# Attention and two feed-forward layers on one core: in the first batch, the f32 products with the values take the two heads of a pair in turn

## The chip, the cores and the metric

One core of one Trainium2 chip. The metric is the device time of one execution in microseconds, lower is better; the number of a kernel is the median of its runs.

## The reference, cut to what matters

```python
# q, k, v: (4 batches, 12 heads, 448 tokens, 64), float32
def attention(q, k, v, g_q, g_k):
    q_n, k_n = rmsnorm(q, g_q), rmsnorm(k, g_k)
    scores = q_n @ k_n.transpose(0, 1, 3, 2) / sqrt(64)
    attn = exp(scores - scores.max(-1, keepdims=True))
    attn = attn / (attn.sum(-1, keepdims=True) + 1e-09)
    return attn @ v                      # the product that the change touches

def reference(...):
    x = attention(...).transpose(0, 2, 1, 3).reshape(1792, 768)
    h = x @ moe_w_in                     # 768 -> 2048
    x = (h / (1 + exp(-1.702 * h))) @ moe_w_out
    h = x @ moe2_w_in                    # 768 -> 2048
    return (maximum(h, 0) + alpha * minimum(h, 0)) @ moe2_w_out
```

The weights come as 64-bit floats and are turned into 32-bit ones on the chip, word by word.

## The kernel before, in words

**Staging.** The first batch (6 pairs of heads) goes through its attention while the weights of the first layer are loaded, converted and split into two f16 parts. Loop `first_pairs` takes units 0 and 1 of each pair (which give the first 256 query tokens) and, between them, the steps of `w1i`, the first weight matrix; the loop after `first_x` takes units 2 and 3 (the other 192 query tokens) with the steps of `w1o`, the second matrix, and with `first_in`, the first layer's product (line 680), which is PE's main load there. From then on attention of the next batch (`other_batches`) is interleaved with the first layer of the batch before (`moe1`), and last comes the second layer.

**A unit of attention.** `scores` multiplies queries and keys of the two heads (line 491, in f32 for the first batch; its two heads lie in the two halves of PE's rows and take turns), DVE takes the maximum (line 505), `exponent` runs the exponential on ACT (line 515), `high` makes a diagonal matrix of the reciprocal sums on ACT (line 529), and `low` transposes the probabilities by a product with that diagonal (line 549, 128 columns a time, f32) and copies them out of PSUM with ACT (line 555) into the tile `ptf`.

**The products with the values.** Function `values(P, half)` (line 585) has, in the first batch, four blocks of 128 (the last of 64) keys for each of the two heads of pair P. Head j's weights are 128 keys by 64 value columns, and its output goes to PSUM partitions 64j to 64j + 63 of the one tile `xp` (one buffer, two heads side by side), so the two heads use different halves of PE's columns. Half 0 streams 256 columns a product, half 1 streams 192. Each f32 product is two instructions on PE in the trace, each with a weight load of its own, so a call of `values` shows as 16 matmuls. In the other batches the operands are f16 and there are 11 products a head, 22 matmuls a call. What follows a call in the first batch is a copy on ACT (line 599, half 0) or a split on ACT and DVE (lines 140 and 141, half 1), which reads both heads.

**Order.** Each engine runs its instructions in the order in which they stand in its queue. That order is made when the program is built, by a planner that plays the program through with its own cost of each instruction, taking what is ready in the order of the code. Loads are issued by SP's queue, in order; a load of weights (line 223) waits there until the buffer it writes has been read.

Of the kernel before, what the change touches and what calls it, by code (L numbers as in the profile page):

```python
# [57 lines left out]
def attention_moe_kernel(  # L58
# [17 lines left out]
    nc = tc.nc  # L76
# [61 lines left out]
    def split(dst, src, scale):  # L138

        nc.scalar.activation(out=dst[0], in_=src, func=AF.Copy, scale=scale)  # L140
        nc.vector.scalar_tensor_tensor(  # L141
            out=dst[1], in0=src, scalar=scale, in1=dst[0], op0=ALU.mult, op1=ALU.subtract
        )
# [426 lines left out]
    def values(P, half):  # L570
        b, p = divmod(P, NP)
        vs = preps[P][1]
        pt = pts.pop((P, half))
        if half == 0 or b == 0:
            xps[P] = ps_x.tile([128, S], F32, tag="x", name="xp")
        xp = xps[P]
        if b == 0:
            steps = [(c, c, slice(64 if c == 3 else 0, 128)) for c in range(NV)]
        else:
            steps = [(c, c, slice(0, 128)) for c in range(7)] + [(c + 7, c, slice(0, 128)) for c in range(4)]  # L580
        parts = PARTS[half]
        for group in (parts,) if b else [(part,) for part in parts]:
            for i, (c, kc, ks) in enumerate(steps):
                for j, o, t, n in group:
                    nc.tensor.matmul(  # L585
                        out=xp[64 * j:64 * j + 64, t:t + n],
                        lhsT=vs[ks, j, c],
                        rhs=pt[ks, kc, o:o + n],
                        start=(i == 0),
                        stop=(i == len(steps) - 1),  # L590
                    )
        if b and half == 0:
            xs[b, p] = big.tile([128, 2, S], F16, tag="x", name="x", bufs=NX)
        elif b:
            x = xs[b, p]
            split((x[:, 0], x[:, 1]), xp, scales["w1i"][1][:, p:p + 1])
        elif half == 0:
            xraw[p] = big.tile([128, S], F32, tag="x", name="xraw", bufs=NX)
            nc.scalar.activation(out=xraw[p][:, 0:FIRST], in_=xp[:, 0:FIRST], func=AF.Copy)
        else:  # L600
            first_split(p, xp, slice(FIRST, S))

    def first_split(p, src, cols):
        x = xs[0, p]
        split((x[:, 0, cols], x[:, 1, cols]), src[:, cols], first_sc[:, p:p + 1])
# [9 lines left out]
    def attention(us):  # L615

        for i in range(len(us) + LAG):
            if 0 < i <= len(us):
                high(us[i - 1])
            if i < len(us):  # L620
                scores(us[i])
                exponent(us[i])
            if 2 <= i <= len(us) + 1:
                low(us[i - 2])
            if i >= LAG and us[i - LAG] % 2 == 1:
                values(us[i - LAG] // 4, us[i - LAG] % 4 // 2)
            yield
# [476 lines left out]
    if True:  # L1104
# [10 lines left out]
        parts = stage[:, 0:R1I * 1024].bitcast(I32).rearrange("p (i n t) -> p i n t", i=R1I, t=2)  # L1115
# [40 lines left out]
        steps = attention([4 * P + r for P in range(NP) for r in range(2, 4)])  # L1156
# [71 lines left out]
```

## Time and profile before

| | |
|---|---|
| median of 3 runs | 1199.72 us (1193.25, 1199.72, 1202.79) |
| profiled execution | 1196.5 us |
| its span, first to last instruction | 1194.7 us |
| PE busy | 1103.3 us (92%) |
| DVE busy | 815.3 us (68%) |
| ACT busy | 685.1 us (57%) |
| granted TensorE clock, mean | 0.971 |

PE is TensorE's matmul stream, PEld its weight loads, DVE VectorE, ACT ScalarE, POOL GpSimd, SP the engine whose queue issues the loads. A granted clock of 1.00 is 2.4 GHz, 0.50 is 1.2 GHz.

### The profile page before, as it was taken

The numbers are of one execution on the slowest core, as the hardware profiler recorded it, in microseconds if no ns is written. First come the engines' busy times: TensorE is split into PE (matmuls) and PEld (weight loads), VectorE is DVE, ScalarE is ACT, GpSimd is POOL, SyncE is SP. The second block draws the span as 40 slices with busy tenths as digits, with TensorE's granted clock in tenths as the row PEclk, the third lists the DMA queues.
The fourth block names the chain that finished last, engine by engine and source line by source line (L and its number), as shares of the span: only waits on it lengthen the run. The fifth ranks groups of instructions, "written<-read, shape, count | busy, mean of one in ns | idle before, by whom it ended". The sixth has DMA issues, their size and how long they took to land.

```text
span 1194.7 us, 18498 instructions
## 1 busy us (share of the span) xinstructions
PE 1103.3 (92%) x6827; PEld 615.2 (51%) x6827; DVE 815.3 (68%) x1433; ACT 685.1 (57%) x1408; POOL 86.1 (7%) x200
## 2 busy tenths in 40 slices
PE   3678999968999988999998999999999999999998
PEld 1444566745544444545544545544444467566665
DVE  6988988898567885457752677489995422978351
ACT  4677878697377875568852445346555322656220
POOL 2320000451101101010000000000000000000000
PEclk9789999978999998999999999999999999999999
DMA  7862555677477675656652741274614413353111
GB/s 239 256 149 80 169 139 119 135 147 166 101 157 142 134 155 111 143 106 114 108 139 63 263 137 51 79 263 175 222 71 151 147 70 126 98 167 104 34 28 33
DMA packets 256459, 158.07 MB, mean 132 GB/s; under 512 B 177648, under 2 KB 239728, under 8 KB 256368
## 3 DMA queue, kind: packets, MB, share of 16 engines
q1 hardware_dynamic: 256368, 156.89, 50.0%
q8 instruction: 53, 0.87, 0.3%
q14 instruction: 38, 0.31, 0.1%
HBM read 92.22 MB, written 25.69 MB: 99 GB/s over the span
## 4 chain that ended last, share of the span: by engine, by line
PE 55%; DVE 16%; DMA 11%; ACT 10%; issue 4%; SPq 2%; POOL 1%; ACTq 0%; DVEq 0%
PE op L1012 13%; PE yp L750 13%; PE h L852 10%; PE hp L727 8%; PE xp L585 5%; ACT pr L515 3%; PE hp L680 2%; DVE nm L505 2%; PE sp L500 2%; DVE ph L560 2%; DMA g<-in_moe_w_in_dram 2%; PE tp L549 1%; DMA yr<-y_dram 1%; PE sp L491 1%; DVE g L141 1%
## 5 line engine op out<-in xcount | busy, mean ns | idle before, releaser
L750 PE MATMUL yp<-g,w1o 128*128 128x448 f16 x1152 | 228.3, 357 | 9.0 <-ACT g L140 4.2
L852 PE MATMUL h<-x,w2i 128*128 128x512 f16 (+1 forms) x1152 | 218.9, 352 | 2.8 <-DVE pos L858 1.7
L750 PEld LDWEIGHTS <-w1o 128*128 128x128 f16 x1152 | 111.3, 99 | 117.1 <-issue 18.8
L727 PE MATMUL hp<-x,w1i 128*128 128x448 f16 x864 | 169.1, 353 | 2.6 <-DVE t L736 2.6
L852 PEld LDWEIGHTS <-w2i 128*128 128x128 f16 x1152 | 112.7, 98 | 108.0 <-issue 3.3
L727 PEld LDWEIGHTS <-w1i 128*128 128x128 f16 x864 | 82.2, 98 | 84.4 <-issue 9.9
L505 DVE TENSOR_REDUCE nm<-sp 128x2 f32<-128x896 f32 x96 | 92.6, 965 | 10.4 <-PE sp L500 9.5
L560 DVE SCALAR_TENSOR_TENSOR ph<-pr,sm,ph 128x448 f16<-128x448 f32 x126 | 83.7, 690 | 19.7 <-ACT ph L534 19.3
L515 ACT ACTIVATE pr<-sp,nm,c_s 128x448 f32<-128x448 f32 x126 | 90.1, 718 | 2.2 <-DVE ph L560 0.8
L857 ACT ACTIVATE pos<-h,sign 128x512 f32<-128x512 f32 (+1 forms) x64 | 40.2, 629 | 86.8 <-PE h L852 80.9
L534 ACT ACTIVATE ph<-pr,sm 128x448 f16<-128x448 f32 x126 | 78.0, 659 | 19.0 <-DVE sm L525 19.0
L1012 PEld LDWEIGHTS <-even 128*128 128x128 f16 x672 | 65.7, 98 | 43.4
L858 DVE SCALAR_TENSOR_TENSOR pos<-h,slope,pos 128x512 f32<-128x512 f32 (+1 forms) x64 | 43.6, 683 | 59.8 <-ACT pos L857 59.7
L680 PE MATMUL hp<-x,w1i 128*128 128x256 f16 (+1 forms) x576 | 65.4, 274 | 2.3 <-ACT ptf L555 1.6
L500 PE MATMUL sp<-t 64*128 64x448 f16 (+1 forms) x432 | 56.7, 363 | 11.2 <-ACT pr L515 10.4
L1012 PEld LDWEIGHTS <-odd 128*128 128x128 f16 x504 | 49.2, 98 | 33.0 <-DVE odd L962 0.6
L585 PE MATMUL xp<-pt,vs 128*64 128x256 f16 (+1 forms) x792 | 52.4, 278 | 13.7 <-DMA pt<-ph 7.2
L1012 PE MATMUL op<-w2lo,even 128*128 128x384 f16 x384 | 63.4, 326 | 0.0
L680 PEld LDWEIGHTS <-w1i 128*128 128x128 f16 x576 | 54.6, 103 | 14.6 <-issue 9.6
L549 PE MATMUL tp<-dg,pr 128*128 128x128 f32 x336 | 51.2, 304 | 10.3 <-ACT dg L529 9.4
L549 PEld LDWEIGHTS tp<-dg,pr 128*128 128x128 f32 x336 | 44.9, 210 | 21.5 <-ACT dg L529 12.8
L141 DVE SCALAR_TENSOR_TENSOR g<-t,ratio_w1o,g 128x448 f16<-128x448 f32 x64 | 44.8, 703 | 16.1 <-ACT g L140 16.1
(220 smaller groups left out, 1597.1 us busy)
## 6 DMA issues: line engine op xcount, KB each, us to landing
g<-in_moe_w_in_dram SPq DMA_DIRECT2D x24, 512.0 KB, 5.4
g<-in_moe_w_out_dram SPq DMA_DIRECT2D x32, 384.0 KB, 4.0
w2raw<-in_moe_w_in_dram SPq DMA_DIRECT2D x24, 512.0 KB, 5.8
w2raw<-in_moe_w_out_dram SPq DMA_DIRECT2D x16, 768.0 KB, 6.5
g_dram<-pos SPq DMA_DIRECT2D x48, 256.0 KB, 2.0
gp<-g_dram SPq DMA_DIRECT2D x8, 1024.0 KB, 6.5
odd<-g_dram SPq DMA_DIRECT2D x6, 1024.0 KB, 5.4
y_dram<-y SPq DMA_DIRECT2D x24, 224.0 KB, 2.2
```

The lines of the kernel that those rows point to most:

```text
L500: nc.tensor.matmul(out=sp[:, j, 0:S] if n == 2 else sp[ds, 0, 0:S], lhsT=qt[ds] if n == 2 else qt[ds, 64:128], rhs=kt[ds, 0:S], start=(i = ...
L505: nc.vector.tensor_reduce(out=nm[:, 0:n], in_=sp[:, 0:n, 0:S], op=ALU.max, axis=AX, negate=True)
L515: nc.scalar.activation(out=pr[i], in_=sp[:, i, 0:S], func=AF.Exp, bias=nm[:, i:i + 1], scale=c_s if u >= 4 * NP else 1.0, accum_out=sm[:, ...
L534: nc.scalar.activation(out=ph[:, i, 0:S], in_=pr[i], func=AF.Copy, scale=sm[:, i:i + 1])
L549: nc.tensor.matmul(out=tp[:, c, i], lhsT=pr[i][:, o:o + 128], rhs=ph[:, i], start=True, stop=True)
L560: nc.vector.scalar_tensor_tensor(out=ph[:, i, S:2 * S], in0=pr[i], scalar=sm[:, i:i + 1], in1=ph[:, i, 0:S], op0=ALU.mult, op1=ALU.subtract)
L585: nc.tensor.matmul(out=xp[64 * j:64 * j + 64, t:t + n], lhsT=vs[ks, j, c], rhs=pt[ks, kc, o:o + n], start=(i == 0), stop=(i == len(steps) ...
L680: nc.tensor.matmul(out=ps, lhsT=w1i[:, kk, e, m * 128:(m + 1) * 128], rhs=xs[0, kk][:, f, cols], start=(i == 0), stop=(i == 3 * KD - 1))
L727: nc.tensor.matmul(out=ps, lhsT=w1i[:, kk, e, m * 128:(m + 1) * 128], rhs=x[:, f], start=(n == 0), stop=(n == 3 * KD - 1))
L750: nc.tensor.matmul(out=ps, lhsT=w1o[:, m, e, j * 128:(j + 1) * 128], rhs=g[:, m, f], start=(n == 0), stop=(n == 3 * KF - 1))
L852: nc.tensor.matmul(out=ps, lhsT=w2i[:, kk, e, m * 128:(m + 1) * 128], rhs=x2[kk][:, f], start=(c == 0), stop=(c == 3 * KD - 1))
L1012: nc.tensor.matmul(out=ps, lhsT=ops[:, o, m, f], rhs=rhs[:, e], start=(c == 0), stop=(c == 3 * KH - 1))
```

## The change

In the first batch, too, `values` goes block by block and takes the two heads in turn within each block, as it does in the other batches. Before, it ran the four blocks of head 0 and then the four of head 1. The products, their operands, their shapes and their number stay the same; their order on PE changes.

```diff
-        for group in (parts,) if b else [(part,) for part in parts]:
-            for i, (c, kc, ks) in enumerate(steps):
-                for j, o, t, n in group:
-                    nc.tensor.matmul(
-                        out=xp[64 * j:64 * j + 64, t:t + n],
-                        lhsT=vs[ks, j, c],
-                        rhs=pt[ks, kc, o:o + n],
-                        start=(i == 0),
-                        stop=(i == len(steps) - 1),
-                    )
+        for i, (c, kc, ks) in enumerate(steps):
+            for j, o, t, n in parts:
+                nc.tensor.matmul(
+                    out=xp[64 * j:64 * j + 64, t:t + n],
+                    lhsT=vs[ks, j, c],
+                    rhs=pt[ks, kc, o:o + n],
+                    start=(i == 0),
+                    stop=(i == len(steps) - 1),
+                )
```

## Rows read from the trace of the kernel before

**Rows 1.** Stages: start:end, length; busy PE, PEld, DVE, ACT, POOL (count); clock, DMA share, GB/s.
```profile
0.00:74.00 74.00, 38.23 (x145) 22.41 (x145) 56.44 (x111) 42.32 (x92) 19.29 (x62) 0.84 0.82 233
74.00:104.90 30.90, 25.38 (x124) 14.94 (x124) 28.93 (x49) 23.35 (x55) 7.68 (x14) 0.89 0.34 101
104.90:137.00 32.10, 28.20 (x157) 16.42 (x155) 27.41 (x65) 26.48 (x64) 0.00 (x0) 1.00 0.55 154
137.00:185.00 48.00, 47.93 (x325) 32.90 (x326) 40.28 (x97) 38.28 (x98) 0.00 (x0) 1.00 0.53 131
185.00:216.00 31.00, 29.41 (x210) 21.08 (x210) 24.41 (x50) 24.53 (x61) 0.00 (x0) 0.94 0.48 126
216.00:300.00 84.00, 65.97 (x606) 46.06 (x605) 76.03 (x147) 67.42 (x164) 36.01 (x54) 0.88 0.73 149
300.00:1194.70 894.70, 868.16 (x5270) 461.44 (x5265) 561.84 (x920) 462.73 (x882) 23.14 (x70) 0.99 0.46 123
```

**Rows 2.** The chain that ended last, 74-104.9, 104.9-137, 137-185, 185-216 us; two of its pieces.
```profile
by line: PE xp L585 23.0%; PE tp L549 14.9%; PE sp L491 14.9%; ACT w1i L179 12.2%; ACT pr L515 10.3%; ACT ptf L555 6.7%; ACT t L443 4.7%; ACT dg L529 3.8%; ACT hl L452 2.7%; ACT g L148 2.3%; issue 1.5%; ACT xraw L599 1.2%; PE qt L440 1.1%; 
...
by line: PE xp L585 22.9%; ACT pr L515 14.1%; DMA g<-in_moe_w_out_dram 10.3%; ACT ptf L555 9.8%; PE tp L549 8.6%; PE sp L491 8.1%; ACT w1i L179 5.9%; ACT w1o L148 5.5%; ACT w1o L179 5.1%; ACT x L140 3.7%; ACT dg L529 3.6%; ACT xraw L599 2.0
...
126.90 3.29 DMA g<-in_moe_w_out_dram
...
by line: PE hp L680 34.3%; PE xp L585 27.3%; PE tp L549 20.5%; PE sp L491 15.6%; DMA g<-in_moe_w_out_dram 8.6%; ACT x L140 0.9%; ACT w1o L148 0.5%; ACT pr L515 0.2%; issue 0.1%; PE pm L120 0.1%
...
184.73 4.12 DMA g<-in_moe_w_out_dram
...
by line: PE hp L680 25.6%; DMA g<-in_moe_w_out_dram 24.1%; PE xp L585 10.7%; ACT w1o L179 10.3%; ACT pr L515 4.6%; ACT ph L534 3.6%; DVE nm L505 3.3%; DVE rm_w1o L245 2.8%; ACT ptf L555 2.5%; DVE g L692 2.4%; ACT vs L140 2.0%; ACT sq L396 1
```

**Rows 3.** Busy us of line 585 alone, by stage, columns PE and PEld, clock, DMA.
```profile
0.00:74.00 74.00, 5.46 (x20) 2.24 (x20) 0.84 0.82 233
74.00:104.90 30.90, 8.32 (x28) 3.27 (x28) 0.89 0.34 101
104.90:137.00 32.10, 12.92 (x48) 5.31 (x48) 1.00 0.55 154
137.00:185.00 48.00, 13.67 (x64) 7.17 (x64) 1.00 0.53 131
185.00:216.00 31.00, 6.91 (x32) 3.54 (x32) 0.94 0.48 126
```

**Rows 4.** PE's timeline, f32 products with the values, head after head.
```profile
158.00 1.19 PE L585 MATMUL xp<-ptf,w1o 128*64 128x192 f32 x6
...
180.77 3.24 PE L585 MATMUL xp<-ptf,w1o 128*64 128x192 f32 x16
```

**Rows 5.** PE's timeline: f32 row pairs, f16 products one by one, f16 column pairs.
```profile
137.07 1.02 PE L491 MATMUL sp<-w1o 64*128 64x448 f32 x4 [0.45 <-ACT pr L515]
...
154.14 2.14 PE L680 MATMUL hp<-x,w1i 128*128 128x256 f16 x18
...
440.41 1.39 PE L585 MATMUL xp<-pt,vs 128*64 128x256 f16 x22
```

**Rows 6.** Weight loads of line 585: f32 (0 to 220 us), f16 (the 22 of rows 5).
```profile
L585 PEld LDWEIGHTS xp<-ptf,w1o 128*64 128x64 f32 x96 | 11.3, 137 | 14.9 <-ACT ptf L555 4.4 <-issue 4.1 <-ACT dg L529 1.9
...
L585 PEld LDWEIGHTS <-vs x22: 106/110/110, 440.4 to 441.4; 128*64 128x64 f16 x22
```

**Rows 7.** Waits from 74 to 216 us (ACT), 74 to 137 us (PE), 100 to 262 us (SP's queue).
```profile
ACT xraw L599 <- PE xp L585: 8.9, 4, 3.1
...
PE tp L549 <- ACT dg L529: 6.6, 5, 2.4
...
SPq L223 <- DVE w1o L165: 59.7, 22, 6.9
```

**Rows 8.** PE's busy us and granted clock in two stretches that follow each other.
```profile
98.06:101.47 3.41, 1.28 (x9) 1.00 0.53 182
101.47:104.89 3.42, 3.42 (x14) 0.50 0.00 0
```

## The prediction

> **What bounds the kernel now.** I began with the busy times by stage, since the edit touches only the first batch's products with the values, which all lie before 216 us. The reader is to see three regimes there [rows 1]. Up to 74 us the DMA engines are busy for 0.82 of the time, at 233 GB/s, and PE for 38.2 of 74 us: the loads set the pace. From 74 to 137 us DVE is nearly full (28.9 of 30.9 us, then 27.4 of 32.1) with PE close behind. From 137 to 185 us PE is full (47.9 of 48.0) and DVE has 7.7 us to spare. From 216 to 300 us DVE leads again (76.0 of 84.0), and from 300 us on PE is busy for 868 of 895 us with work that the edit leaves alone.
>
> Next the chain that ended last, stage by stage: line 585 has 23.0% of the first 30.9 us, 22.9% of the next 32.1, 27.3% of 48 and 10.7% of 31, which is 7.1, 7.3, 13.1 and 3.3 us, 30.8 in all [rows 2]. So the products sit on the path, but ACT's lines and two loads of the second weight matrix stand between them. Last the timeline of single calls, to see how PE spends those pieces.
>
> **What a call costs now, and after.** A call with 192 columns takes 3.24 us for its 16 matmuls, and its first six take 1.19 us [rows 4]: the ten others add 2.05 us, 0.205 us each, and the six are 1152 columns at 1.03 ns a column. So the passes run one after the other; while one head's stream, the other half of PE's columns does nothing. Part of the 0.205 us are the steps into and out of the block of 64 keys, which heads in turn meet half as often.
>
> What happens when two heads take turns is not in the trace for f32 in column halves, so I bound it by two neighbours [rows 5]. The f16 products with the values, in later batches, take turns in just this way: 22 matmuls of 256 columns in 1.39 us, 0.247 ns a column, where f16 products of the same 256 columns that go one by one take 2.14 us for 18, 0.464 ns a column. Taking turns brings that to 0.53 of it. In f32 the scores take turns between halves of PE's rows: four passes of 448 columns in 1.02 us, 0.57 ns a column, 0.55 of the 1.03 above. So f32 passes, too, overlap when their parts of the array differ. I take full pairing; the other end, no pairing, is the fourth case below.
>
> A paired call of 192 columns has eight steps in place of sixteen: 3.24 - 8 x 0.2 = 1.6 us, or 0.53 x 3.24 = 1.7 by the f16 rows. Over all 12 calls line 585 is busy for 5.46 + 8.32 + 12.92 + 13.67 + 6.91 = 47.3 us before 216 us [rows 3]; at 0.53 to 0.5 of it **22 to 24 us** leave PE, 20 of them after 74 us. Nothing is added: the same matmuls and loads, no new wait, no DMA. One wait moves: the passes that need only the first of the two transposed copies are now those of both heads, eight instead of four, so less is left behind the second copy. I cost that at nothing; it helps only where PE waits for ACT.
>
> **How much of it reaches the end.** On the chain the 30.8 us of line 585 halve to 15.4 (to 0.5, since a piece of the chain is cut off where the next begins); that is the ceiling, since a call that is off the chain gives nothing. What is next late is DVE, whose own work doesn't shrink, and ACT's chain through exponent, diagonal and copy. By stage:
> - Before 74 us loads set the pace [rows 1]: 0.
> - 74 to 104.9 us: 7.1 us of the chain are line 585, half is 3.6, but DVE has 2.0 us free in all. I take 1.5.
> - 104.9 to 137 us: 7.3 us, half 3.7; DVE has 4.7 free, and ACT waits 8.9 us in four goes for exactly these products before its copy of line 599 [rows 7], so ACT can start earlier. A load of weights stands on the chain at 126.9 us [rows 2]; it waits for a buffer that DVE frees [rows 7], not for PE. I take 2.5.
> - 137 to 185 us: 13.1 us, half 6.6. PE is full, DVE has 7.7 us and ACT 9.7 us free. I take 4.5, as DVE would have to be busy for 40.3 of 41.4 us for all of it.
> - 185 to 216 us: 3.3 us, half 1.7; the chain goes through a load (184.7 us, 4.1 us long [rows 2]), and one of the two calls is off it. I take 1.0.
>
> The sum is **9.5 us**. It should stay: from 216 to 300 us DVE's and ACT's work, earlier as a whole, has no other deadline, and after 300 us PE's work is what it was. DVE and PE from 74 to 300 us are both busy for 197 of 226 us [rows 1]; with the 9.5 us gone DVE would be at 91%, about what it reaches from 216 to 300 us (0.905), which is why I stop there and not at 15. (ACT stays at 0.83 or less in every stage.)
>
> The profiled execution took 1196.5 us, so 1187.0 by its own time, 0.8% less. The median of the three runs lies 0.3% above that execution; the same share of 1199.7 us gives **1190 us**.
>
> **Unknowns with two ends.** The clock: after a stretch with PE busy for 1.28 of 3.41 us it was granted at 0.50 (1.2 GHz) for the next 3.42 us, in which PE was full [rows 8]. With less PE time between 74 and 137 us such a stretch can come once or twice more, at up to 1.7 us each (half of 3.42), or fall elsewhere and spare one: -1.7 to +3.4, and I take 0, inside the rounding of the stages. The planner: it plays another order through and may place a load or a transpose otherwise in SP's queue, where weight loads wait for 59.7 us in 22 goes, up to 6.9 us [rows 7]. The two loads on the chain are 3.3 and 4.1 us; both moved is 7.4 us to either side. I take 0.
>
> **The rivals.** First, everything passes: the slack of DVE and ACT lies where it is needed and the 15.4 us come out whole, 1196.5 - 15.4 = 1181.1, 1184 by the median. For it speaks that from 137 to 185 us four lines of PE make up 97.7% of the chain [rows 2]; against it DVE's 28.9 of 30.9 us before [rows 1].
>
> Second, the gain is eaten: DVE and the chain of ACT (PE already waits 6.6 us for the diagonal between 74 and 137 us [rows 7]) take over at once, and one or two stretches at 1.2 GHz come on top. What is left is 0 to 4 us: 1195 by its own time, 1198 by the median.
>
> Third, on the other side: the weight loads. Each f32 pass has a load of 137 ns [rows 6], hidden now behind the pass before it on the same columns. If in f32 a load for one column half had to wait until the other half's pass had streamed, the 16 loads of a call would add 16 x 0.137 = 2.2 us, less some 0.2 for the steps at the block of 64 met half as often: 2.0 us more for each of 12 calls, some 9.5 of them on the chain, 19 us in full, since time added on the chain is not absorbed: 1215.5 by its own time, 1219 by the median. It decides from the point where a load shows for longer than overlapping passes spare in each step, half a step or 0.1 us. Against it: the 22 f16 loads of 0.11 us each are 2.4 us of loading within 1.39 us of products [rows 5, 6], so there loads run beside both halves' passes; only f32 is open.
> The Trainium skill ("TensorE: Matmul & The Clock Gate", Part 3, under The mechanism) states such a rule: a weight load overlaps a matmul in flight only when the two use different row groups, and here both heads use the same rows. By that rule this change is a loss; this trace's f16 rows, with the same shape of array, do not follow it.
>
> Fourth, the change doesn't do what it says: f32 passes in column halves stay one after the other. Then only the steps at the block of 64 are fewer, at the 0.2 us a call of the case before 1.9 us on the chain: 1194.6, 1198 by the median.
>
> **How the numbers follow.** Forecast (5 to 13 us gained) 0.47; everything passes 0.22; eaten 0.19; no pairing 0.05; loads exposed 0.04; the planner's order costs more than the pairing gives 0.03. About 1%, 12 us, is what a measurement of this kernel can tell from no change. Faster by more is the second number and a quarter of the first, 0.33; slower by more is the loads and half of the planner, 0.06; the rest, 0.61. The range goes from full passage with the planner's 7 us on top, 1177, to the eaten case with some of the planner's cost, 1204.
>
> **What would show it.** In the changed trace the 16 matmuls of a 192-column call should stand in one row of 1.6 to 1.9 us, line 585's f32 calls should be busy for 23 to 27 us in all, ACT's wait for it at line 599 should fall from 8.9 to about 4 us, and DVE should be above 90% from 74 us to the end of the first batch. The forecast is wrong if the row stays above 2.5 us (no pairing), exceeds 3.3 us (loads), or if the row is short and the main products of line 680 still end at 215 us (eaten), or already by 200 us (all passes).

## The result, and the profile after

The changed kernel took 1184.73 us (median of 4 runs, 1183.25 to 1186.04) beside 1198.95 us of the kernel before: a ratio of 0.9885, 95% interval 0.9843 to 0.9927. The profiled execution took 1186.04 us, 10.5 us less than the one before (1196.5).

Lines of the code after the changed place have numbers one lower: 584 for 585, 679 for 680, 749 for 750. First the stages of the changed kernel, with the columns and bounds of [rows 1]:

```profile
0.00:74.00 74.00, 36.69 (x141) 22.66 (x141) 55.34 (x111) 40.98 (x88) 19.30 (x62) 0.79 0.82 226
74.00:104.90 30.90, 25.63 (x132) 15.78 (x134) 30.34 (x50) 25.41 (x61) 8.66 (x14) 0.78 0.38 119
104.90:137.00 32.10, 25.22 (x168) 15.92 (x164) 29.74 (x74) 28.79 (x73) 0.00 (x0) 0.95 0.56 159
137.00:185.00 48.00, 46.45 (x356) 32.25 (x353) 41.86 (x99) 39.21 (x100) 0.00 (x0) 1.00 0.59 154
185.00:216.00 31.00, 27.88 (x246) 21.12 (x246) 26.75 (x50) 24.63 (x62) 5.50 (x13) 0.96 0.47 113
```

DVE is busy for 98% and 93% of the two stages from 74 to 137 us, and for 87% of the next, where it was at 84%: it is now the engine with the least room all the way from 74 to 137 us. Before, PE had been ahead of it between 104.9 and 137 us (28.2 us busy for 27.4); there PE fell to 25.2 us. From 137 us on PE is still the fuller one (46.5 of 48.0 us). Line 584 alone, with the columns of [rows 3]; the f32 calls now end at 201.8 us:

```profile
0.00:74.00 74.00, 3.37 (x16) 1.33 (x16) 0.79 0.82 226
74.00:104.90 30.90, 6.92 (x36) 2.58 (x38) 0.78 0.38 119
104.90:137.00 32.10, 6.49 (x46) 2.29 (x42) 0.95 0.56 159
137.00:185.00 48.00, 8.93 (x64) 4.12 (x64) 1.00 0.59 154
185.00:201.80 16.80, 3.56 (x32) 1.84 (x32) 1.00 0.35 88
```

That is 29.3 us in all, after 47.3. The last call, in PE's timeline, beside [rows 4], and the group of its f32 weight loads, beside [rows 6]:

```profile
200.08 1.67 PE L584 MATMUL xp<-ptf,v 128*64 128x192 f32 x16
```

```profile
L584 PEld LDWEIGHTS xp<-ptf,v 128*64 128x64 f32 x48 | 2.8, 136 | 3.6 <-ACT ptf L555 1.3 <-ACT w1o L148 0.7 <-ACT sm L520 0.7
```

Sixteen matmuls in 1.67 us where they took 3.24. The loads are as long as before, 136 ns, but 48 of them now cover 2.8 us in all, where one after the other they would be 6.5: the two heads' loads overlap too. The chain that ended last from 74 to 202 us, and three of its pieces:

```profile
by line: DMA g<-in_moe_w_out_dram 18.1%; PE tp L549 14.1%; PE hp L679 8.2%; PE xp L584 7.9%; PE sp L491 7.5%; ACT pr L515 5.4%; ACT ptf L555 4.3%; ACT w1o L179 3.9%; DVE w1i L180 3.6%; DVE w1o L180 2.9%; ACT w1o L148 2.9%; ACT dg L529 2.5%;
...
113.89 4.02 DMA g<-in_moe_w_out_dram
...
153.76 5.12 DMA g<-in_moe_w_out_dram
...
187.71 3.38 DMA g<-in_moe_w_out_dram
```

The products have gone from about a quarter of the chain in three of the stages [rows 2] to 7.9%, and what has come up is the loads of the second weight matrix, 18.1%, which wait in SP's queue for DVE as they did before. ACT's wait ahead of the copy (line 598 now), from 74 to 205 us, beside 8.9 us in [rows 7], and the loads' wait from 100 to 262 us, beside 59.7 us there:

```profile
ACT xraw L598 <- PE xp L584: 1.1, 1, 1.1
...
SPq L223 <- DVE w1o L165: 58.5, 24, 6.0
```

### The profile page after: what moved, and what is told of

The parts are those of the page before. It is cut to its first block, busy times and chain, and to the rows that moved or that the text cites. A ratio compares the mean times of both kernels' runs of the same rounds, so it can differ in the third digit from the quotient of the medians.

```text
span 1184.3 us, 18511 instructions
## 1 busy us (share of the span) xinstructions
PE 1083.9 (92%) x6827; PEld 607.1 (51%) x6827; DVE 816.2 (69%) x1433; ACT 684.6 (58%) x1408; POOL 83.0 (7%) x200
## 4 chain that ended last, share of the span: by engine, by line
PE 40%; DVE 20%; DMA 13%; ACT 13%; issue 6%; SPq 4%; POOL 3%; POOLq 0%; ACTq 0%; DVEq 0%
PE op L1011 16%; PE h L851 8%; PE yp L749 6%; PE hp L726 5%; ACT pr L515 4%; DVE ph L560 3%; DVE nm L505 3%; DMA g<-in_moe_w_out_dram 2%; DMA yr<-y_dram 2%; PE xp L584 2%; ACT ph L534 2%; PE tp L549 2%; DMA qk<-in_q_dram 1%; DVE g L141 1%; SPq L566 1%
## 5 line engine op out<-in xcount | busy, mean ns | idle before, releaser
L856 ACT ACTIVATE pos<-h,sign 128x512 f32<-128x512 f32 (+1 forms) x64 | 40.1, 629 | 85.2 <-PE h L851 75.5
L534 ACT ACTIVATE ph<-pr,sm 128x448 f16<-128x448 f32 x126 | 78.0, 661 | 18.4 <-DVE sm L525 18.3
L679 PE MATMUL hp<-x,w1i 128*128 128x256 f16 (+1 forms) x576 | 62.1, 265 | 13.9 <-DVE t L691 10.0
L549 PE MATMUL tp<-dg,pr 128*128 128x128 f32 x336 | 55.3, 321 | 14.7 <-ACT dg L529 13.3
L549 PEld LDWEIGHTS tp<-dg,pr 128*128 128x128 f32 x336 | 48.6, 225 | 27.0 <-ACT dg L529 16.8
L507 ACT ACTIVATE nm<-nm,c_s 128x2 f32<-128x2 f32 x72 | 20.9, 290 | 65.5 <-DVE nm L505 65.5
```

Of the source, the lines that this page charges most:

```text
L534: nc.scalar.activation(out=ph[:, i, 0:S], in_=pr[i], func=AF.Copy, scale=sm[:, i:i + 1])
L549: nc.tensor.matmul(out=tp[:, c, i], lhsT=pr[i][:, o:o + 128], rhs=ph[:, i], start=True, stop=True)
L679: nc.tensor.matmul(out=ps, lhsT=w1i[:, kk, e, m * 128:(m + 1) * 128], rhs=xs[0, kk][:, f, cols], start=(i == 0), stop=(i == 3 * KD - 1))
```

## The experiments

Two theories stood at the start: that the pairing shortens the chain and with it the end; and that the end moved because the planner, which plays the whole program through, put the queues of all engines into another order. In the traces, each of the first four edits below and the change itself put other instructions into some 200 to 550 places of the queues of PE, DVE and ACT, the first of them between 56 and 148 us and the last before 480 us, even where an edit pairs nothing.

**One half at a time, and head 1 first.** Edits of the line that the change removed (first three runs), or of the changed loop (the fourth):

```diff
half0_turns
-        for group in (parts,) if b else [(part,) for part in parts]:
+        for group in (parts,) if b or half == 0 else [(part,) for part in parts]:
half1_turns
+        for group in (parts,) if b or half == 1 else [(part,) for part in parts]:
head1_first_no_turns
+        for group in (parts,) if b else [(part,) for part in parts[::-1]]:
head1_first_turns (in the changed kernel)
-            for j, o, t, n in parts:
+            for j, o, t, n in parts if b else parts[::-1]:
```

> Only the calls of half 0 (256 columns, 55 to 133 us) take the heads in turn. Theory 1, PE's time on the chain: the f32 calls of half 0 fall from 4.3 to 2.3 us, those of half 1 stay at 3.2 to 3.5, and the end moves by what the stage before 137 us gave in the changed kernel, whose last copy of line 599 ended 3 us earlier: 3 to 5 us faster. Theory 2, the planner's other order of the other engines does it: the two halves alone need not add up to the 14 us of both, and this one may come out anywhere between 14 us faster and 7 us slower.

> Only the calls of half 1 (192 columns, 142 to 213 us) take the heads in turn. Theory 1: those calls fall from 3.2 to 3.5 us to 1.7 to 2.4, half 0 stays at 4.3, and the end comes 6 to 9 us earlier, since PE is full from 137 to 185 us; with the run of half 0 alone it adds up to what both gave. Theory 2: no such sum.

> Both halves in turn, but head 1 ahead of head 0 in each block: the same pairing, another order made by the planner (several hundred places of DVE's and ACT's order differ from the changed kernel's). Theory 1: the same calls (1.7 to 2.4 us) and 10 to 15 us faster than before. Theory 2: another time than the changed kernel's by more than 5 us.

> Head after head as before, but head 1 ahead of head 0: no pairing, calls stay at 3.2 to 4.3 us, and only the planner's order changes, in as many places as the change itself makes. Theory 1: within 3 us of before. Theory 2: several us to one side, 5 or more.

| run | median us | ratio, 95% interval |
|---|---|---|
| half0_turns | 1205.57 | 1.0033 (1.0012 to 1.0053) |
| half1_turns | 1205.01 | 1.0027 (1.0013 to 1.0041) |
| head1_first_turns | 1195.93 | 0.9943 (0.9914 to 0.9972) |
| head1_first_no_turns | 1203.33 | 1.0002 (0.9982 to 1.0022) |

The first theory, as it was put, fell here: each half alone makes the kernel a little slower, where it should have given 3 to 9 us, and the same pairing with the heads the other way round gives half of what the change gives. An order that changes without any pairing moved nothing, so the second theory did not come out in full either. Half 1's own calls did get shorter: 1.9 to 2.4 us of PE for 3.2 to 3.7. In the trace of half1_turns a call of half 0 from 74 to 85 us met a low clock, ahead of the first place in which its queues differ from those of the kernel before. Line 585 in that stretch, columns PE, PEld, clock, DMA, of the kernel before (12 of the call's 16 passes; the other four had run from 72.9 us on, in 1.08 us) and of half1_turns (all 16):

```profile
74.00:85.00 11.00, 4.01 (x12) 1.50 (x12) 0.84 0.47 147
```

```profile
74.00:85.00 11.00, 7.92 (x16) 2.81 (x16) 0.53 0.56 174
```

That is 7.9 us for 5.1 in these two executions. The changed kernel has a low clock there too (0.78 from 74 to 104.9 us), so this is no cost of the edit.

**Fewer joints; fewer passes.** The heads take turns every two blocks; or the order of before with three blocks of head 1 left out:

```diff
two_blocks_a_turn
+        runs = [[s] for s in steps] if b else [steps[0:2], steps[2:4]]
+        for run in runs:
+            for j, o, t, n in parts:
+                for c, kc, ks in run:
                     nc.tensor.matmul(
...
head1_one_block (in the kernel before)
+            mine = steps if b or group[0][0] == 0 else steps[0:1]
-            for i, (c, kc, ks) in enumerate(steps):
+            for i, (c, kc, ks) in enumerate(mine):
```

> The heads take turns every two blocks in place of every block. Passes of different column halves are then next to each other only at the joints, two or three a call. If a pass can only overlap with its neighbour in the order, a call has 13 or 14 steps in place of 16 or 8: 2.7 to 2.8 us with 192 columns, and 3 to 5 us of the 14 are gained. If PE looks further ahead in its queue, a call falls to 1.7 us as in the changed kernel and the whole 14 us come.

> Order of before, but head 1 gets only its first block of keys (its last three are left out): 10 passes in place of 16, one after the other, no pairing, about 2.0 us with 192 columns. Theory 1, it is PE's time and not the turns as such: three quarters of the gain, 7 to 12 us faster than before. Theory 2, the new order does it: no gain beyond 3 us.

two_blocks_a_turn: 1204.85 us, 1.0021 (1.0007 to 1.0034). head1_one_block: 1203.23 us, 1.0010 (0.9993 to 1.0027). Both miss what the first theory asked of them: in the second run six of sixteen passes are gone from each call, and nothing comes of it at the end. What the turns every two blocks do to a call is below.

**DVE's work.** Two of DVE's three steps on each piece of the first layer's weights are left out, in the kernel before and in the changed one:

```diff
-        nc.vector.tensor_scalar(out=bits, in0=bits, scalar1=3, ...)
-        nc.vector.scalar_tensor_tensor(out=bits, in0=lo, scalar=29, ...)
+        if "w1o" in scales:
+            (the same two)
```

> The kernel before with two of DVE's steps on each piece of the first layer's weights left out (the shift by three bits and the one that puts in the low word): some 55 us of DVE's work between 24 and 220 us are gone. If DVE is what holds the stages from 74 us on beside PE: 4 to 12 us faster than before. If PE alone holds them: within 3 us of before.

> The changed kernel with the same two steps of DVE left out. If DVE, next late, keeps part of the pairing's 15 to 20 us from the end: this one is faster than the kernel before with the same steps left out by 14 us or more, and 20 us or more faster than before. If loads or ACT's chain keep it: 8 to 12 us apart from the other, as with all of DVE's work.

before_less_dve: 1193.42 us, 0.9918 (0.9890 to 0.9947). after_less_dve: 1192.91 us, 0.9907 (0.9882 to 0.9931). So these steps (44.9 us of DVE's busy time, 815.3 less 770.4; 55 were expected) are worth 9 us of the end, as forecast. With them gone the medians of the two kernels differ by 0.5 us in place of 14; by the two intervals it can be anything from some 3 us slower to 6 us faster, so the 14 us are not there, but that the pairing gives nothing is not shown. The stages of the two runs (first before_less_dve; bounds at 137 us and where the last f32 call ends):

```profile
74.00:137.00 63.00, 52.09 (x279) 31.10 (x278) 44.29 (x92) 52.85 (x127) 4.68 (x14) 0.94 0.49 141
137.00:202.60 65.60, 65.60 (x475) 47.72 (x474) 39.14 (x80) 50.84 (x130) 0.00 (x0) 1.00 0.47 112
```

```profile
74.00:137.00 63.00, 49.29 (x294) 31.50 (x295) 46.24 (x94) 54.36 (x132) 6.61 (x14) 0.89 0.50 141
137.00:197.20 60.20, 57.85 (x457) 42.42 (x455) 37.65 (x76) 49.45 (x128) 0.00 (x0) 0.97 0.49 115
```

The f32 calls end 5.4 us earlier, in a stretch in which PE had been full and DVE at 60%. Of that, 3.0 us are left where the conversion's last step starts (211.2 for 214.2 us) and 0.6 at the first product of the next sum (273.1 for 273.7), so it is lost behind 197 us. But the two kernels also differ in the order of their queues (272 places of PE's, 312 of DVE's, 399 of ACT's), and which of the two eats it these runs can't tell.

**The order of the queues, held.** To part the two theories, every engine's queue was held to a given order with ordering edges between neighbours. The traces show the orders held: PE's 6827, DVE's 1433 and ACT's 1408 instructions stand in the same order of lines as in the kernel that the order is from. That the edges cost no time is borne out by after_moved below, whose queues are held in this way and which is as fast as the changed kernel. The names in `ORDER` are places in the program as it is traced, which all these kernels share; within a call the k-th place goes to the k-th product.

```diff
+    traced = list(tc.nc.cur_bb.bb.instructions)
+    info = mybir.DependencyInfo(mybir.DependencyClass.NoSync, mybir.DependencyReason.DATA)
+    for places in ORDER:                 # one list for each engine
+        for a, b in zip(places, places[1:]):
+            tc.add_manual_dep(traced[b], traced[a].name, info, reason="order of another build")
```

turns_in_old_order is the changed kernel with the queues of the kernel before; two_blocks_in_new_order is the kernel of two_blocks_a_turn with the queues of the changed one.

> The heads take turns in both halves, but every engine's queue is held, place by place, to the order that the planner made for the kernel before; within a call the k-th place goes to the k-th product. Only the pairing differs from before. Theory 1, the pairing makes the gain and the planner's other order only adds or takes a little: the last f32 call ends 8 to 11 us earlier, and the end comes 7 to 14 us earlier. Theory 2, the order of the queues after 200 us makes it: the f32 calls end earlier all the same, but the weights' conversion still ends at 224 to 226 us, DVE still stands 8 us behind a score product at about 320 us, and the end is within 4 us of before.

> The other way round: every engine's queue is held to the order of the changed kernel, but the heads take turns only every two blocks, so that calls stay at 2.7 to 2.8 us with 192 columns (3.2 before, 1.7 in the changed kernel). Theory 1: a third of the pairing's gain, 2 to 5 us faster than before. Theory 2: most of the changed kernel's gain, 10 to 14 us, since the order is the same.

| products | queues of before | own queues | queues of the changed kernel |
|---|---|---|---|
| heads apart | 1 | 1 | - |
| turns every two blocks | - | 1.0021 (1.0007 to 1.0034) | 0.9945 (0.9924 to 0.9966) |
| turns every block | 0.9966 (0.9953 to 0.9979) | 0.9885 (0.9843 to 0.9927) | the same |

The medians of the two new runs are 1196.58 and 1193.83 us, beside 1200.72. Down a column only the products differ, along a line only the order. With the order of before, pairing is worth 0.34%, 4.1 us (0.21 to 0.47%). With the order of the changed kernel, going from turns every two blocks to every block is worth 0.6%, some 7 us, with nearly as much uncertainty (0.1 to 1.1%, worked out from the two intervals). The order is worth 0.8%, some 9 to 10 us, for either kind of turns (0.4 to 1.2% and 0.5 to 1.0%). Both runs came out between what the theories forecast: the old order left 4.1 us of the 7 to 14 that the first asked for, and the new order gave the turns every two blocks 6.9 us, where 2 to 5 or 10 to 14 were expected. The free place (heads apart in the new order) can't be filled: that order puts products of both heads ahead of a transpose that head 0's third block needs.

Every two blocks a call takes 2.59 us for 192 columns, between the 3.24 and the 1.67 of the other two, here in PE's timeline of two_blocks_in_new_order. Below it are the two parts of a call with 256 columns: blocks 1 and 2 of both heads, then blocks 3 and 4; then the same parts in the changed kernel; then blocks 1 and 2 of head 0 alone in the kernel before:

```profile
205.41 2.59 PE L586 MATMUL xp<-ptf,v 128*64 128x192 f32 x16
...
88.21 1.09 PE L586 MATMUL xp<-ptf,w1o 128*64 128x256 f32 x8
90.52 2.37 PE L586 MATMUL xp<-ptf,w1o 128*64 128x256 f32 x8
```

```profile
89.05 1.08 PE L584 MATMUL xp<-ptf,w1o 128*64 128x256 f32 x8
91.32 1.23 PE L584 MATMUL xp<-ptf,w1o 128*64 128x256 f32 x8
```

```profile
87.58 1.08 PE L585 MATMUL xp<-ptf,w1o 128*64 128x256 f32 x4
```

Blocks 1 and 2 pair in full although the four passes of head 0 stand ahead of the four of head 1 in the queue: eight passes in 1.09 us, as long as four of one head alone. (The trace doesn't name a pass's half; eight one after the other would take twice as long.) So PE started passes of the other column half from four places further on. In the second part nothing pairs (2.37 us for 1.23); there head 0's block of 64 keys stands between the full blocks of the two heads. The expectation had put a shorter call down to passes overlapping at the joints alone; the time came near it (2.59 for 2.7 to 2.8), the mechanism is another.

Now where the order acts. The conversion of the second weight matrix ends with the last step of line 180, and the first batch's second product (tile `yp`) can start when everything that hangs on it is split. Two rows each, first and last start and the count, of the kernel before, turns_in_old_order, the changed kernel and two_blocks_in_new_order:

```profile
L180 DVE SCALAR_TENSOR_TENSOR w1o<-num1o,inv_w1o,w1o x2: 1007/1022/1036, 224.6 to 225.6; 128x768 f16<-128x768 f32 x2
L750 PE MATMUL yp<-g,w1o x42: 349/353/581, 288.4 to 298.7; 128*128 128x448 f16 x42
```

```profile
L180 DVE SCALAR_TENSOR_TENSOR w1o<-num1o,inv_w1o,w1o x2: 1010/1014/1018, 220.6 to 221.5; 128x768 f16<-128x768 f32 x2
L749 PE MATMUL yp<-g,w1o x55: 352/353/577, 284.5 to 299.9; 128*128 128x448 f16 x55
```

```profile
L180 DVE SCALAR_TENSOR_TENSOR w1o<-num1o,inv_w1o,w1o x2: 1007/1736/2464, 221.1 to 223.4; 128x768 f16<-128x768 f32 x2
L749 PE MATMUL yp<-g,w1o x127: 352/352/363, 274.5 to 300.0; 128*128 128x448 f16 x127
```

```profile
L180 DVE SCALAR_TENSOR_TENSOR w1o<-num1o,inv_w1o,w1o x2: 1004/1736/2467, 224.0 to 226.4; 128x768 f16<-128x768 f32 x2
L751 PE MATMUL yp<-g,w1o x102: 352/353/582, 278.6 to 299.8; 128*128 128x448 f16 x102
```

With the ends of the last f32 call, here of the kernel before and of turns_in_old_order, the marks are (us, one execution each):

```profile
210.31 2.59 PE L585 MATMUL xp<-ptf,v 128*64 128x192 f32 x12
```

```profile
207.23 1.34 PE L584 MATMUL xp<-ptf,v 128*64 128x192 f32 x12
```

| kernel | last f32 call ends | conversion's last step starts | first `yp` product starts |
|---|---|---|---|
| before | 212.9 | 225.6 | 288.4 |
| turns_in_old_order | 208.6 | 221.5 | 284.5 |
| two_blocks_a_turn | 210.3 | 223.8 | 284.2 |
| two_blocks_in_new_order | 208.0 | 226.4 | 278.6 |
| the changed kernel | 201.8 | 223.4 | 274.5 |
| half0_turns | 209.7 | 226.0 | 297.0 |
| half1_turns | 212.1 | 227.1 | 297.4 |

In the old order the pairing brings the three marks forward by 4.3, 4.1 and 3.9 us, as much as the medians gain. (The profiled executions do not show it at the end, 1198.0 us for 1196.5: they vary by several us, as the runs do.) From the conversion's last step to the first `yp` product it is 62.8 and 63.0 us in the old order, and 51.1 and 52.2 in the new one, whatever the pairing. But the new order takes longer ahead of that: from the last f32 call to the conversion's last step 21.7 and 18.4 us, after 12.7 and 13.0. Over both, the new order is only 3 to 5 us shorter (72.8 and 70.6 for 75.5 and 75.9). So of the 10 us that the order brings the first `yp` product forward where the heads take turns every block, 6.8 lie ahead of the end of the f32 calls and 3.1 behind it; for turns every two blocks it is 2.2 and 3.3, and the rest of that gain lies behind the mark. In the two runs with one half the first `yp` product comes 9 us later than before, and what makes it late lies behind the f32 calls (87.3 and 85.3 us for 75.5).

The stretch from the conversion's end to the first `yp` product, in the sequence of the rows above, with the columns of [rows 1]:

```profile
226.60:288.40 61.80, 43.77 (x427) 31.48 (x424) 54.66 (x104) 51.84 (x129) 29.04 (x39) 0.86 0.75 150
```

```profile
222.50:284.50 62.00, 43.92 (x425) 31.65 (x422) 55.96 (x105) 52.17 (x129) 29.39 (x40) 0.83 0.73 149
```

```profile
224.50:274.50 50.00, 34.57 (x361) 26.27 (x361) 48.22 (x95) 42.45 (x107) 17.05 (x21) 0.90 0.79 159
```

```profile
227.40:278.60 51.20, 37.41 (x361) 29.05 (x361) 49.05 (x97) 43.85 (x110) 18.08 (x22) 0.84 0.81 161
```

DVE is nearly full in it (88% to 96%) and PE, with 70%, waits; PE has 427 and 425 matmuls there in the old order and 361 in the new. The difference is attention of the next batch. Its score products in the same stretch, kernel before and changed kernel, and then the same and the products with the values in the stretch from the last f32 call to the conversion's end:

```profile
L500 PE MATMUL sp<-t x78: 346/349/578, 226.5 to 284.3; 64*128 64x448 f16 x60, 64*64 64x448 f16 x18
```

```profile
L500 PE MATMUL sp<-t x54: 346/349/577, 226.6 to 269.7; 64*128 64x448 f16 x36, 64*64 64x448 f16 x18
```

```profile
L500 PE MATMUL sp<-t x14: 349/349/373, 220.3 to 226.5; 64*128 64x448 f16 x8, 64*64 64x448 f16 x6
L585 PE MATMUL xp<-pt,vs x1: 297/297/297, 221.7 to 221.7; 128*64 128x256 f16 x1
```

```profile
L500 PE MATMUL sp<-t x24: 349/359/577, 207.7 to 222.2; 64*128 64x448 f16 x18, 64*64 64x448 f16 x6
L584 PE MATMUL xp<-pt,vs x42: 246/282/423, 212.1 to 223.3; 128*64 128x256 f16 x22, 128*64 128x192 f16 x20
```

78 score products against 54 behind the conversion, but 14 against 24 ahead of its end: about half of the difference is done earlier, and twelve score products, two units of six, are left for later, under the long `yp` sums where PE is full and DVE and ACT have room. The products with the values that are missing behind the conversion (90 for 131) have all moved ahead of its end (42 for 1). So DVE has 48.2 us of work behind the conversion, for 54.7, and ACT 42.5 for 51.8.

**A score product left behind.** In the old order DVE stands for 9.7 us at about 320 us for one product of PE. Waits of turns_in_old_order from 195 to 370 us, and PE's timeline:

```profile
DVE nm L505 <- PE sp L500: 11.1, 3, 9.7
```

```profile
297.35 0.35 PE L500 MATMUL sp<-t 64*128 64x448 f16 x1
297.64 21.74 PE L749 MATMUL yp<-g,w1o 128*128 128x448 f16 x114
319.31 0.36 PE L500 MATMUL sp<-t 64*128 64x448 f16 x1
```

The sixth product of a unit comes 22 us after its fifth. I moved it, and in another run the parted unit of the changed kernel's own order (places in the queue of PE, and of DVE in the second; `sp` is a score product, `pm` the product for the maximum over partitions, `nm` DVE's maximum over the scores, `qk` the scaling of queries and keys):

```diff
turns_old_order_moved (queues of before)
  sp 1 to 5, 
+ sp 6, 
  yp x73, 
+ yp of the next sum x1, pm, 
  yp x29, ... yp x11, 
- sp 6, pm
after_moved (queues of the changed kernel)
  sp 1, yp x2, sp 2, yp x102, sp 3 to 6   ->   sp 1 to 6, yp x104
  DVE: ... qk, qk, nm of this unit        ->   ... nm of this unit, qk, qk
```

> The turns in the order of the kernel before, with three products of PE moved forward in its queue: the sixth score product of one unit, which stood behind 113 products of line 749 while its five siblings ran 22 us earlier, comes behind those; and the product of the partition maximum comes 34 places earlier, with the first product of the sum that must be allotted ahead of it. If this one place in the order costs the end what DVE waits there: DVE's wait of 9.7 us at 320 us goes to 2 us or less, and the end comes 4 to 9 us earlier than with the turns in the old order, 8 to 13 us faster than before. If the wait is hidden, since PE is busy all through it: within 2 us of the turns in the old order, 3 to 5 us faster than before.

> The changed kernel in its own order, with five score products of one unit, which stand behind 102 products of line 749, moved to the unit's first two, and DVE's maximum over them moved ahead of the two steps that wait for GpSimd at 302 to 306 us. If a unit's products that the planner parts cost the end: 2 to 6 us faster than the changed kernel, 0.984 to 0.987 of before. If they are covered by GpSimd's wait: the same as the changed kernel, 0.986 to 0.993.

turns_old_order_moved: 1195.66 us, 0.9955 (0.9941 to 0.9968), not told apart from 0.9966. It did not test what it was to test: DVE's maximum ran at 309.3 us, but the next one then waited as long, for the next unit's products, which stand behind the rest of the same sums. DVE's and PE's timelines:

```profile
309.27 1.08 DVE L505 TENSOR_REDUCE nm<-sp 128x2 f32<-128x896 f32 x1
...
320.36 0.62 DVE L505 TENSOR_REDUCE nm<-sp 128x1 f32<-128x448 f32 x1 [9.06 <-PE sp L500]
```

```profile
309.63 10.00 PE L749 MATMUL yp<-g,w1o 128*128 128x448 f16 x52
319.56 0.76 PE L500 MATMUL sp<-t 64*64 64x448 f16 x6
```

after_moved: 1185.16 us, 0.9864 (0.9841 to 0.9887): the same as the changed kernel within both intervals. It lies in both forecasts' ranges, is the lowest ratio of the study and no proven gain over the change.

## Why the prediction was right, point by point

- **The call.** 1.6 to 1.7 us was forecast and 1.67 measured; f32 passes in column halves pair in full. The fourth rival (no pairing) and the third (loads that show) are out: 16 loads of 136 ns are 2.2 us, and the call takes 1.67. So the rule of the Trainium skill ("TensorE: Matmul & The Clock Gate", Part 3, The mechanism), by which a load overlaps a matmul in flight only with another row group, does not hold for these f32 products, whose row groups are the same. The rows before the change had spoken against it too: without overlap, 137 of a pass's 205 ns would be its load, which leaves 0.35 ns a column, less than the 0.46 of the f16 products that go one by one [rows 4, 5, 6].
- **PE's time.** 22 to 24 us were forecast, 18.0 measured (47.3 less 29.3). The term was too large: calls that the planner parts with transposes pair less (1.9 to 2.4 us in place of 1.67 for five of the six with 192 columns), and the call from 74 us on took 4.15 us in place of 2.31 at a lower clock (0.78 in place of 0.89 from 74 to 104.9 us). So line 584 was busy for 29.3 us, where 23 to 27 were the sign.
- **How much reaches the end of the f32 calls.** 9.5 us by stages, for the pairing alone. In the changed kernel the last f32 call ended at 201.8 us for 212.9, 11.2 us earlier, but that is pairing and order together: with the order held, the pairing brought 4.3 us. (Counted from the start of the second call, which that execution reached 2.6 us late, it is 6.9.) So the sum of the stages was too large for what it stood for; which stage's share was, the two traces don't tell. DVE was forecast above 90% up to the end of the first batch; it was at 98% and 93% up to 137 us, then at 87% and 86%. ACT's wait at the copy fell to 1.1 us, further than the 4 of the forecast.
- **"It should stay."** With the order held this step was right: 4.3 us at the end of the f32 calls, 3.9 at the first `yp` product, 4.1 by the medians. Where the planner orders anew it is not safe: the half-way edits lost all that they had gained, and in the changed kernel the conversion's last step started only 2.2 us earlier (223.4 for 225.6). The first `yp` product came 13.9 us forward; 3.9 of these come with the pairing alone, the other 10 with the order.
- **The planner**, which I took at 0 with 7.4 us to either side, is the mis-sized term. Its order was worth 9 to 10 us, more than the pairing alone (4.1 us in the old order). It came out on the good side. With one half, or with turns every two blocks, the kernel was 2.7 to 3.3 us slower than before in spite of the pairs; for the turns every two blocks the held order shows that this is the planner's doing, for the halves it is inferred. The forecast of 9.5 us by the profile and 10 by the median against 10.5 and 14.2 is thus partly luck: pairing in a fixed order would have given 4, about the upper end of what the prediction called eaten (0 to 4). By the median the kernel even came out at the first rival's time (1184 for everything passes), and not for its reason.
- **DVE as what is next late** was half right. Its work is worth time, as before_less_dve shows with 9 us; but without it the pairing's gain did not grow, so no run shows that DVE's work on the weights is what kept it from the end. Which of the moved products make the order's 9 to 10 us is not shown; no run moved just these. That is left open, as is where after_less_dve loses its gain behind 197 us.

## What to carry to other kernels

Products whose outputs need no more than 64 partitions can run side by side in the two column halves, in f32 as in f16: here turns every block halved PE's time for a call that nothing parts (3.24 to 1.67 us), and took 47.3 to 29.3 us over all calls. Turns every two blocks did as well among blocks of 128 keys, but not across a block of 64. But where a planner orders the queues, an edit of one loop is an edit of all queues: hold the order fixed, both ways, before crediting the time to the edit. And time taken off one engine in a stretch that another one closes is only a chance; look at what ends the stretch (here the conversion of the weights, then DVE ahead of the long sums) and at which work could be left for a later stretch in which that engine has room.

## What the runs showed of the hardware that was not expected

Turns every two blocks pair in full among blocks of 128 keys: eight passes in 1.09 us, where turns every block take 1.08 and four passes of one head 1.08. So, other than said of all engines at the start, PE did not start these passes strictly in the order of its queue; it started those of the other column half four places ahead of their turn. Across the block of 64 keys it did not (2.37 us for 1.23). That the block's other number of rows is the reason is a guess, and whether head after head would pair with the two short blocks put last was not run. Two executions can differ by some us through the granted clock in one call: with the same products and the same order of the queues up to there, the last twelve passes of the second call of half 0 took 4.01 us of PE in the kernel before and 5.95 in half1_turns, in a stretch granted at 0.84 and 0.53.
